# One core, TensorE-bound: the last 64 columns of a weight matrix on both halves of the array, with small loads, stores and the whole order redone

## The chip, the cores and the metric

The kernel runs on one core of one Trainium2 chip. The metric is the device time of the kernel in microseconds (us): a median of several runs. The profiles show one execution each. Engines: PE is TensorE's matmuls, PEld its weight loads, DVE is VectorE, ACT is ScalarE, POOL is GpSimd, SP is SyncE, which here only issues DMAs.

## What is computed

Two branches share a layer norm, and are multiplied and added at the end. S = 2048 rows, D = 640, F = 1728, all in bfloat16.

```python
x  = A_q
xn = layernorm(x)
# A: a 4-tap shift of k, times v, then a long causal convolution along S by FFT
k_shift = sum(k_pad[:, t:t + S, :] * shift_k[:, ks - 1 - t] for t in range(ks))
kv = k_shift * v
y  = irfft(rfft(kv, 2 * S) * rfft(ssm_k, 2 * S))[:S] + kv * ssm_D
s  = xn * y
# B: a feed-forward layer
h  = gelu(xn @ w1 + b1)          # w1: 640 x 1728
g  = silu(h @ w2 + b2)           # w2: 1728 x 640
return x + s * g
```

## The kernel before

Rows of x lie 16 to a partition (partition p holds rows 16p to 16p + 15), which makes 16 groups `n` of 128 rows; four groups make a chunk `c`, so there are four chunks of 512 rows. All row buffers of 640 values are slots of one SBUF tile `mem`; PSUM is one tile `ps` of eight banks.

The order of all work on all engines is one string, `PLAN`. Each word is a step: a name, `/row` for the slot where its result lies, `@bank` for its PSUM bank or banks, and `~a` or `~d` for the engine that evacuates it (ScalarE or VectorE). The steps are recorded in that order, and each engine executes its own instructions in it. The words that matter here:

- Feed-forward, layer 1: `h{c}_{ft}` (`ffn1`, L451) multiplies one tile of 128 columns of w1 (14 tiles, `ft` 0 to 13) with the turned chunk of x, five matmuls of 512 columns that add up over the 640 inputs. In chunk 0 six of the tiles are done in two halves, `ha` and `hb`, of 256 columns. `he` (`ffn1_out`, L456) applies the bias and Gelu into `hT`. F = 1728 is 13 x 128 + 64, so tile 13 holds 64 true columns; the other 64 of its weights are zeros set by `ones_row` (step `mh`).
- Layer 2: `g{c}_{i}` (`ffn2`, L466), 14 matmuls of 320 columns each; i // 2 is the group in the chunk, i % 2 the half of the 640 outputs. The 14th uses 65 rows: 64 of h, and a row of ones against b2, which is row 64 of the last tile of `w2_sb`. Then `ge` (Silu, L471) and `gm` (product with xn, L475).
- Convolution, as a two-stage transform of length 4096 by matmuls: `kf`, `uf` (`mm2`, L197) for the first stage of filter and input, with stores `ks`, `us` to HBM on the POOL queue and loads `fl`, `ml` back on the SP queue; `ff`, `mu` (`mm8`, L207) for the second, `mp` (`product`, L544) the product of the spectra, `mc`, `md` (also L207) back, `ms` a store to HBM, `yl` a load, `y` (`inv2`, L583) the last stage. `mm8` runs one operation as eight matmuls on 32x32 pieces of the array: for each of two halves of the columns, four pieces on one diagonal. The diagonal follows from g: even g use two of the four, odd g the other two.
- Evacuations from PSUM are at L191 (ScalarE) and L192 (VectorE).
- Start: `xl0_0`, `xl0_1` load chunk 0 of x in two halves; `st` (L405, L406) takes the statistics of one group, `sq` and `rc` make the reciprocal root for two groups, `nm` (L421) norms one, `tx` (L426) turns it, `te0_*` evacuates it. `em` (L351) turns the four taps of shift_k, `ee` evacuates them. `wu` and `wv` are matmuls without use that keep TensorE busy.
- k with its shift: `klh` and `kl` load k; row 0 of the three halo slots must be zero, which `k_zero` (steps `kz0` and `kz1`, L280) writes on ScalarE.
- Loads of the feed-forward weights: `wa` (w1 by columns), `wb0` (w2's 13 whole tiles), `wb1` (its last 64 rows, and b2), all on SP.
- End: `yc` (L587) evacuates `y`, `yt` (L592) gates it, `yo` (L598) adds x, and `os` (L603) stores a group, or half of one, on SP.

Of the kernel before, what the change touches and what calls it, by code (L numbers as in the profile page):

```python
# [11 lines left out]
BF16 = mybir.dt.bfloat16  # L12
I32 = mybir.dt.int32
ACT = mybir.ActivationFunctionType
ALU = mybir.AluOpType

P = 128
# [17 lines left out]
ws0/77 st1_1 hb1 h0_13@5 wb1 st1_3 h0_11@2 he0_1 st1_2 xl2/81 h0_10@6 s rs1 kl1 he0_11 h0_12@0 he0_3 he0_2 it0@2  # L35
vl0/85 it1@4 he0_10 hb0 d he0_13 nm1_1 kt1@7 nm1_3 he0_12 kt0@6 nm1_2 em2@5 nm1_0 he0_0 vl1/89 kc1/58~d tt1_0@0
ee2~a ie0/59~d tt1_2@1 tt1_1@7 te1_0/93~d te1_2~a kt8@2 kl2 ss h0_6@5 te1_1~d ie1~d kt2@7 ee3~d kf1_0@0.1 xl3/97
ha4@4 he0_6 kc0/16~d ha5@3 cm0_2/63 hb4 kc2/17~d hb5 cm0_1/101 ke1_0/103~a kf0_0@6.7 h0_8@5 he0_5 cm0_0/105
ke0_0/107~a cm1_0/109 kf2_0@0.1 h0_7@3 he0_8 cm1_1/18 ke2_0/20~a ca0_1 kt9@5 he0_4 kf1_1@6.7 h0_9@0 kc9/22~d ke1_1~a
cm0_3/101 he0_7 kl3 kt3@1 kc8/58~d vl2/65 kt4@4 he0_9 kf2_1@6.7 sm kf0_1@2.3 ke2_1~a ca0_2 g0_0@5 kc3/39~a vl3/0  # L40
cm1_3/4 ke0_1~a ca0_3 kt6@0 ge0_0/0 st2_3 kf3_0@6.7 g0_1@1 st2_1 ke3_0/6~a st2_0 kc4/40~a kt5@5 kt7@2 kc5/17~a
kf3_1@6.7 g0_6@3 st2_2 kc6/16~a ge0_1/1 ca1_1 rs2 ke3_1~a cm1_2/63 kt10@4 ge0_6/2 kf4_1@0.1 kc10/41~a kf4_0@6.7 cv0
g0_3@5 kc7/101~a ks3 nm2_2 nm2_3 ke4_0/18~a nm2_0 ke4_1~a ca1_2 kf5_0@2.3 kf7_0@6.7 kf5_1@0.1 ca1_3 ke7_0/39~a
g0_5@4 cv1 ke5_0/85~a ke5_1~a nm2_1 cm2_1/63 kf7_1@6.7 uf0_0@2.3 gm0_6 g0_4@0 gm0_1 ue0_0/4~a cm2_0/87 ge0_5/2
ke7_1~a cm2_2/6 ge0_3/1 uf1_1@2.3 ks7 ca2_1 uf1_0@6.7 kf6_0@4.5 ks1 cm2_3/101 g0_2@1 ue1_0/63~a ue1_1~a ca2_2
ke6_0/42~a us1 gm0_3 gm0_0 uf2_0@6.7 ge0_4/1 cm3_0/6 ks4 uf0_1@2.3 ge0_2/0 uf3_0@4.5 ks5 ue2_0/39~a ue0_1~d kt14@0
kt15@1 ue3_0/105~a uf3_1@6.7 kc14/17~d kf6_1@2.3 kc15/44~d ue3_1~a kf8_0@4.5 gm0_2 kf8_1@0.1 ke8_0/103~a ke6_1~d
kt11@6 kt12@7 ke8_1~a kc11/110~d kf9_0@4.5 uf2_1@2.3 ca2_3 kc12/16~a kf9_1@0.1 g0_7@6 ke9_0/63~a cv2 ke9_1~a
cm3_1/18 ue2_1~a kf11_0@4.5 ca3_1 ge0_7/0 kf10_1@0.1 kf10_0@2.3 ke11_0/85~a h1_0@7 cm3_3/101 ke10_0/89~a cm3_2/18
ke10_1~a kf11_1@4.5 uf4_0@2.3 he1_0 ke11_1~d h1_1@6 ue4_0/109~d ks11 kf12_0@0.1 uf5_0@4.5 ks0 ca3_2 kt13@2 he1_1  # L50
h1_2@3 us2 ue5_0/45~d ke12_0/18~a ks6 kc13/58~d kf12_1@6.7 ks9 he1_2 kf14_0@4.5 ca3_3 uf4_1@0.1 ks10 ke14_0/22~a
h1_3@2 ke12_1~d us0 ue4_1~a ks2 cv3 uf5_1@4.5 he1_3 it2@3 cm4_1/24 kf13_0@6.7 ue5_1~a kf13_1@0.1 h1_7@2 ke13_0/26~a
cm4_0/28 us5 ke13_1~a us4 cm4_2/30 kf15_0@4.5 uf6_0@6.7 ks13 h1_12@0 cm4_3/32 ue6_0/34~a ks8 ca4_1 ke15_0/36~a us3
it3@1 he1_7 ie2/38~d uf6_1@6.7 ks12 h1_4@4 ue6_1~a ca4_2 ie3~a h1_10@5 ca4_3 he1_4 cv4 uf7_1@2.3 he1_10 uf7_0@6.7
h1_9@1 cm5_1/101 ue7_0/107~a cm5_0/85 ue7_1~a kf15_1@4.5 kf14_1@6.7 cm5_2/87 ke15_1~a h1_5@2 ke14_1~a ca5_1 ks15
h1_8@3 he1_12 ks14 ca5_2 he1_5 us7 uf9_0@4.5 cm5_3/63 he1_8 uf8_0@6.7 us6 h1_11@0 he1_9 ca5_3 ue9_0/4~a h1_6@1 cv5
he1_11 fl0/91 cm6_2/89 fl6/30 h1_13@2 he1_6 fl4/32 gm0_5 fl1/42 ue8_0/109~d uf8_1@4.5 fl3/6 he1_13 uf11_0@0.1 fl2/26
ue8_1~d uf11_1@6.7 fl7/24 ue11_0/65~a tt2_0@3 fl10/44 gm0_4 uf9_1@4.5 ue11_1~a cm6_1/46 uf10_0@0.1 g1_2@2
te2_0/101~a fl12/16 cm6_0/105 ue9_1~a cm7_0/18 fl9/20 ue10_0/87~a ca6_1 ff1@6.7 ff0@4.5 fl8/48 uf10_1@0.1 fe0/36~a
g1_0@3 ca6_2 ge1_2/2 fl5/63 ue10_1~d cm7_1/22 ff12@4.5 ff13@0.1 fe1~a g1_6@2 cm6_3/67 ge1_0/1 ca7_1 fe12/107~a  # L60
fe13~a gm1_0 ca6_3 ff2@6.7 ff3@4.5 ff4@0.1 mk6/95 g1_5@3 cm7_3/93 fe2/34~a fe4/28~a mk0/57 cv6 fe3~a cm7_2/91
fl14/46 uf12_1@6.7 ge1_5/1 mk1/85 uf12_0@0.1 ca7_2 uf13_0@4.5 ue12_0/89~a g1_1@3 gm0_7 fl11/30 ca7_3 ue13_0/50~a
ge1_6/0 cv7 ue12_1~a uf13_1@0.1 st3_2 ff6@4.5 us12 ff7@6.7 g1_3@2 ue13_1~a us11 fe6/22~a st3_0 us8 fe7~a us10 gm1_6
gm1_5 uf14_0@0.1 ge1_3/0 st3_3 uf14_1@4.5 g1_4@6 ue14_0/42~a ue14_1~a gm1_2 st3_1 ge1_1/1 us14 uf15_0@0.1 ge1_4/2
# [24 lines left out]
yl11/30 yl2/32 yl10/18 g3_1@1 yl8/87 ge3_5/1 yl0/89 ge3_2/0 y15@4.5 yl9/91 ge3_1/2 y4@6.7 yc15 gm3_1 y13@0.1 yl7/2
yc4 y14@4.5 yc13 yl5/4 yt4 g3_7@2 yt15 yc14 yo4 yl1/16 ge3_4/2 yt14 yt13 yl6/105 y3@6.7 gm3_2 gm3_4 ge3_7/0 y12@0.1  # L90
# [8 lines left out]
def kernel(  # L99
# [76 lines left out]
    def flat(name, n, o=0):  # L176
        return rows(name, n, o).rearrange("p a b -> p (a b)")
# [490 lines left out]
```

## Time and profile before

| | us |
|---|---|
| median of 3 runs | 202.63 (201.66 to 203.36) |
| the profiled execution | 201.33 |
| its span, first to last instruction | 199.5 |
| granted TensorE clock, mean | 0.994 of full |

| engine | busy us | instructions |
|---|---|---|
| PE | 189.4 (95%) | 2194 |
| DVE | 175.7 (88%) | 304 |
| ACT | 155.1 (78%) | 242 |
| POOL | 39.9 (20%) | 71 |

The profile's page lists busy times, the chain of waits that ended last (followed back from the last instruction), and groups of like instructions with their mean duration and the idle time before them. A line number is that of the kernel; L191, L192, L197 and L207 are helpers that many steps share. Matmuls are pipelined: the mean duration of one (299 ns for 320 columns) is longer than the distance from one start to the next.

### The profile page before, as it was taken

To read this page: it belongs to the slowest core of one execution; us is meant where nothing else is said; L and a number is where in the kernel's file an instruction comes from. 1 tells how busy PE (TensorE), PEld (TensorE's weight loads), DVE (VectorE), ACT (ScalarE), POOL (GpSimd) and SP (SyncE) were. 2 spreads that over 40 slices of the span, in tenths; PEclk is the share of its full clock that TensorE was granted. 3 is DMA by queue.
4 is the path that set the end of the run, shared out by engine and by line. 5 is a ranking of instruction groups with operands and counts; after the bars stand their busy time and mean duration, and the time that the engine had idled before them with its cause. 6 is when DMAs were issued, how large, how long until landed. Compare 5 with 4: busy or idle time off the path is not lost.

```text
span 199.5 us, 5511 instructions
## 1 busy us (share of the span) xinstructions
PE 189.4 (95%) x2194; PEld 114.7 (57%) x2194; DVE 175.7 (88%) x304; ACT 155.1 (78%) x242; POOL 39.9 (20%) x71
## 2 busy tenths in 40 slices
PE   2999999999999999999999999999999999999990
PEld 0685867777766555666743344666654433677760
DVE  7999999999999999999888999888999898009992
ACT  5899999987999998998788778535858767547850
POOL 8402000232308621002620000000062632100000
PEclk9999999999999999999999999999999999999997
DMA  5999999982607979999967999997868492599983
GB/s 209 383 415 334 323 347 405 414 328 75 263 0 276 374 287 320 311 374 324 359 247 225 320 347 375 305 292 292 260 229 306 144 312 89 162 333 402 371 301 137
DMA packets 27120, 57.71 MB, mean 289 GB/s; under 512 B 2966, under 2 KB 16983, under 8 KB 27094
## 3 DMA queue, kind: packets, MB, share of 16 engines
q1 hardware_dynamic: 23072, 41.62, 60.0%
q0 software_dynamic: 3840, 15.73, 21.3%
q8 instruction: 17, 0.28, 0.6%
q14 instruction: 9, 0.07, 0.1%
q10 hardware_dynamic: 182, 0.01, 0.1%
HBM read 33.76 MB, written 18.35 MB: 261 GB/s over the span
## 4 chain that ended last, share of the span: by engine, by line
PE 86%; ACT 3%; issue 3%; DVE 3%; DMA 2%; ACTq 1%; DVEq 0%
PE ps L466 30%; PE ps L451 29%; PE ps L197 9%; PE ps L207 7%; PE ps L583 4%; PE ps L483 3%; ACT mem L191 2%; DMA prm<-in_A_ssm_D_dram 2%; PE ps L432 1%; DVE mem L544 1%; DVE mem L192 1%; PE ps L563 1%; PE ps L351 1%; ACT L471 1%; ACT sl L471 0%
## 5 line engine op out<-in xcount | busy, mean ns | idle before, releaser
L191 ACT CAST mem<-ps 128x640 bf16<-128x640 f32 x101 | 67.0, 699 | 13.8 <-PE ps L207 10.2
L451 PE MATMUL ps<-mem,w_sb 128*128 128x512 bf16 (+1 forms) x310 | 67.8, 359 | 0.4 <-ACT mem L191 0.2
L466 PE MATMUL ps<-w_sb,hT 128*128 128x320 bf16 x448 | 65.8, 299 | 0.2
L466 PEld LDWEIGHTS <-hT 128*128 128x128 bf16 x448 | 42.9, 98 | 18.9 <-issue 1.7
L544 DVE TENSOR_TENSOR mem<-ps,mem 128x1280 bf16<-128x1280 f32 x32 | 46.1, 1486 | 3.6 <-PE ps L207 1.8
L451 PEld LDWEIGHTS <-w_sb 128*128 128x128 bf16 x310 | 28.3, 98 | 27.7 <-issue 4.4
L456 ACT ACTIVATE hT<-ps,b_f 128x512 bf16<-128x512 f32 (+1 forms) x56 | 36.9, 693 | 2.9 <-PE ps L451 2.6
L471 ACT ACTIVATE sl<-ps 128x320 bf16<-128x320 f32 x32 | 13.9, 443 | 16.9 <-PE ps L466 13.6
L502 DVE TENSOR_TENSOR mem<-mem 128x1280 bf16<-128x1280 bf16 x32 | 25.1, 821 | 0.0
L192 DVE CAST mem<-ps 128x640 bf16<-128x640 f32 x27 | 21.7, 821 | 3.0 <-PE ps L207 1.7
L558 POOL DMA_DIRECT2D scrC<-mem x16 | 11.4, 715 | 58.1 <-ACT mem L191 56.5
L207 PE MATMUL ps<-mem,mats 32*32 32x320 bf16 x1024 | 22.6, 300 | 0.4 <-DVE mem L544 0.2
L197 PE MATMUL ps<-mem 128*128 128x320 bf16 x128 | 22.7, 299 | 0.0
L505 DVE TENSOR_TENSOR mem<-mem 128x1280 bf16<-128x1280 bf16 x24 | 19.6, 819 | 0.2
L207 PEld LDWEIGHTS <-mats 32*32 32x32 bf16 x1024 | 9.8, 88 | 15.9 <-issue 13.5
L475 DVE TENSOR_TENSOR mem<-mem,sl 128x320 bf16<-128x320 bf16 x32 | 9.4, 316 | 9.2 <-ACT sl L471 9.0
L197 PEld LDWEIGHTS <-mem 128*128 128x128 bf16 x128 | 12.0, 98 | 5.9
L405 DVE BATCH_NORM_STATS2 stats<-mem 128x6 f32<-128x320 bf16 x32 | 13.6, 468 | 0.0
L518 POOL DMA_DIRECT2D scrU<-mem x16 | 8.7, 545 | 22.3 <-ACT mem L191 21.4
L191 ACT COPY mem<-ps 128x640 bf16<-128x640 bf16 (+2 forms) x16 | 11.4, 746 | 1.7 <-DVE mem L544 0.8
L496 POOL DMA_DIRECT2D scrK<-mem x16 | 8.8, 556 | 19.0 <-ACT mem L191 10.0
L192 DVE COPY mem<-ps 128x640 bf16<-128x640 bf16 (+2 forms) x21 | 11.4, 578 | 0.3 <-PE ps L426 0.3
(75 smaller groups left out, 141.8 us busy)
## 6 DMA issues: line engine op xcount, KB each, us to landing
scrK<-mem POOLq DMA_DIRECT2D x16, 320.0 KB, 3.8
scrU<-mem POOLq DMA_DIRECT2D x16, 320.0 KB, 5.4
mem<-scrK SPq DMA_DIRECT2D x16, 320.0 KB, 6.0
mem<-mem SPq DMA_DIRECT2D x32, 160.0 KB, 5.6
mem<-scrU SPq DMA_DIRECT2D x16, 320.0 KB, 6.8
scrC<-mem POOLq DMA_DIRECT2D x16, 320.0 KB, 4.1
mem<-scrC SPq DMA_DIRECT2D x16, 320.0 KB, 6.5
mem<-in_A_q_dram SPq DMA_DIRECT2D x7, 640.0 KB, 4.6
```

The lines of the kernel that those rows point to most:

```text
L191: return nc.scalar.copy(out=out_ap, in_=in_ap)
L192: return nc.vector.tensor_copy(out=out_ap, in_=in_ap)
L197: nc.tensor.matmul(out=o[:, h, :], lhsT=lhsT, rhs=rhs[:, h * HALF:(h + 1) * HALF], start=start, stop=stop)
L207: nc.tensor.matmul(out=o[j, h, :], lhsT=m[i, i], rhs=rhs[i, h * HALF:(h + 1) * HALF], start=start, stop=stop)
L405: nc.vector.bn_stats(out=stats[:, n, h, :], in_=x_row(n)[:, h * HALF:(h + 1) * HALF])
L451: nc.tensor.matmul(out=bank(hname(c, ft))[:, a:b], lhsT=w1_sb[:, t, ft * P:(ft + 1) * P], rhs=rhs, start=(t == 0), stop=(t == DT - 1))
L456: nc.scalar.activation(out=hT[0:M, ft, :], in_=bank(hname(c, ft))[0:M, :], func=ACT.Gelu_apprx_tanh, bias=b1_f[0:M, ft:ft + 1], scale=1.0)
L466: nc.tensor.matmul(out=bank(f"g{c}_{i}")[:, 0:HALF], lhsT=hT[0:M, ft, q * P:(q + 1) * P], rhs=w2_sb[0:M, ft, hs], start=(ft == 0), stop=(f ...
L471: nc.scalar.activation(out=at["sl", c, i], in_=bank(f"g{c}_{i}")[:, 0:HALF], func=ACT.Silu)
L502: nc.vector.tensor_tensor(out=rows(f"cm{i}_{j}", 2), in0=rows("kz0", 2, 3 + 2 * i - j), in1=taps(j), op=ALU.mult)
L505: nc.vector.tensor_tensor(out=rows(f"cm{i}_0", 2), in0=rows(f"cm{i}_0", 2), in1=rows(f"cm{i}_{j}", 2), op=ALU.add)
L544: nc.vector.tensor_tensor(out=rows(f"mp{g}", 2).rearrange("p k (h c) -> p k h c", h=2), in0=banks(f"mu{g}")[:, None, :, :].to_broadcast([P ...
```

## The change

- Layer 1, tile 13 (`ffn1_last`): the 64 true columns of w1 are loaded twice, into columns 0 to 63 and 64 to 127 of the array. The first copy works on the chunk's first 256 rows of x, the second on the other 256, and the results land in partitions 0 to 63 and 64 to 127 of the bank. `ffn1_out` evacuates that tile by two instructions of 64 x 256.
- Layer 2: for groups 2 and 3 of a chunk the 14th matmul takes all 128 rows: row 0 is ones, rows 1 to 63 zeros (set once by `ones_row`), rows 64 to 127 hold h. `w2_sb` has a 15th tile for it, the last 127 rows of w2 under a row of b2.
- b2 is loaded by two DMAs on POOL's queue (`wb2`); SP's `wb1` loads 64 and 127 rows of w2.
- The halo's zero row is one DMA on SP, from the zero columns of `w1_sb`; the two ScalarE instructions leave.
- Four of the 17 stores of the output (groups 10, 12, 5 and 1) are issued on ScalarE's queue.
- `mm8` takes its pair of diagonals from a table, `SIDE`, that differs from g % 2 for some of the g from 16 on.
- The whole `PLAN` is new: order, slots, banks, and the evacuating engine of some 25 steps. The input loads now begin `xl0_0 xl0_1 xl1 cl0 wa0 cl1`, with `kz0` behind them.

The old and new starts of PLAN, and the core of the rest:

```diff
-io1/0 dm qs xl0_0/8 xl1/12 id pd/16 xl0_1 wa0 wa2 qr cl0/23 cl1 w cl2 io2 wu@0 kz0/39 cl3 st0_0 ws1/58 mh cl4 st0_1
-pt@1 em0@2 wa1 pb sq0 em3@3 kz1 rc0 wv1 nm0_0 nm0_1 tx0@4 st0_2 tx1@5 te0_0/65~a em1@6 klh st0_3 te0_1~a wv1
-ee0/69~a ha2@7 ee1~d ha0@1 sq1 ws2/73 rc1 ha1@0 nm0_2 nm0_3 tx2@2 tx3@6 kl0 te0_2~d ha3@4 te0_3~d st1_0 hb3 wb0 hb2
+io1/0 dm qs xl0_0/8 xl0_1 id pd/12 xl1/34 cl0/38 wa0 qr cl1 w io2 wu@0 st0_0 ws1/19 mh st0_1 pt@1 em0@2 kz0/54 st0_3
+sq0 em1@3 wa2 ee0/73~a cl2 wv3 rc0 st0_2 cl3 cl4 wa1 nm0_0 sq1 ws2/26 rc1 tx0@4 nm0_1 em3@5 nm0_2 tx1@6 te0_0/77~d
+em2@7 nm0_3 tx2@2 te0_1~d tx3@0 pb ha1@4 te0_3~d klh st1_0 ha0@6 ws0/30 ha2@1 kl0 te0_2~d ha3@0 st1_1 hb0 it0@2
...
-g3_6@4 yc6 yo5 os7 yt1 os5 yt6 yo1 yo6 ge3_6/0 os1 os6 gm3_6 yo12_0 yo15_0 os15_0 os12
+gm3_0 os9 y1@6.7 yo13_1 yo12_0 yc6 os14 yt5 g3_6@2 os13 yc1 yt6 yo5 os12~a yt1 os5~a yo6 yo1 ge3_6/0 os6 gm3_6 os1~a
+yo15_0 os15_0
...
+SIDE = "01010101010101011001101000111001"
...
-            turn = 2 * (g % 2) + h
+            turn = 2 * int(SIDE[g]) + h
...
-        nc.gpsimd.memset(hT[FLAST:FLAST + 1, FT - 1, :], 1.0)
+        nc.gpsimd.memset(hT[FLAST:FLAST + 1, FT - 1, 0:2 * P], 1.0)
+        nc.gpsimd.memset(hT[0:FLAST, FT - 1, 2 * P:4 * P], 0.0)
+        nc.gpsimd.memset(hT[0:1, FT - 1, 2 * P:4 * P], 1.0)
...
     def k_zero(i):
-        nc.scalar.activation(out=flat("kz0", 3)[0:1, i * 960:i * 960 + 960], in_=spare[0:1, 0:1].to_broadcast([1, 960]),
-                             func=ACT.Copy, scale=0.0)
+        nc.sync.dma_start(out=flat("kz0", 3)[0:1, :].rearrange("o (a t c) -> o a t c", a=6, t=DT),
+                          in_=w1_sb[0:6, :, F:FT * P])
...
     def load_w2_end():
         nc.sync.dma_start(out=w2_sb[0:FLAST, FT - 1, :], in_=B_w2[(FT - 1) * P:F, :])
-        nc.sync.dma_start(out=w2_sb[FLAST:FLAST + 1, FT - 1, :], in_=B_b2.rearrange("(o d) -> o d", o=1))
+        nc.sync.dma_start(out=w2_sb[1:P, FT, :], in_=B_w2[F - P + 1:F, :])
+
+    def load_b2():
+        for p, ft in ((FLAST, FT - 1), (0, FT)):
+            nc.gpsimd.dma_start(out=w2_sb[p:p + 1, ft, :], in_=B_b2.rearrange("(o d) -> o d", o=1))
...
+    def ffn1_last(c):
+        ft = FT - 1
+        for t in range(DT):
+            for j in range(2):
+                o, s = slice(FLAST * j, FLAST * j + FLAST), slice(2 * P * j, 2 * P * j + 2 * P)
+                nc.tensor.matmul(out=bank(hname(c, ft))[o, s], lhsT=w1_sb[:, t, ft * P:F], rhs=x_turned(c)[:, t, s],
+                                 start=(t == 0), stop=(t == DT - 1))
...
-            M = P if ft < FT - 1 else FLAST + 1
+            up = ft == FT - 1 and q >= 2
+            M = FLAST + 1 if ft == FT - 1 and not up else P
             nc.tensor.matmul(out=bank(f"g{c}_{i}")[:, 0:HALF], lhsT=hT[0:M, ft, q * P:(q + 1) * P],
-                             rhs=w2_sb[0:M, ft, hs], start=(ft == 0), stop=(ft == FT - 1))
+                             rhs=w2_sb[0:M, ft + up, hs], start=(ft == 0), stop=(ft == FT - 1))
...
-    def out_store(n, h=None):
+    def out_store(n, h=None, eng=None):
+        if h == "a":
+            h, eng = None, "a"
         hs = slice(0, D) if h is None else half_of(h)
-        nc.sync.dma_start(out=out_v[:, n, hs], in_=x_row(n)[:, hs])
+        (nc.scalar if eng else nc.sync).dma_start(out=out_v[:, n, hs], in_=x_row(n)[:, hs])
```

More of the change, by code (lines that the diff above doesn't have):

```diff
@@ L36 @@
[L36 to L40, printed above, removed]
@@ new lines @@
+kc2/18~d he0_6 kl1 ie1~d kt1@5 kt5@0 kc1/19~d hb4 kc9/20~d h0_8@1 cm0_0/93 cm1_0/95 kf0_0@6.7 ha5@3 ke0_0/97~a
+cm0_2/99 kf1_0@4.5 hb5 he0_4 kc5/101~d kf2_0@6.7 ke1_0/102~a cm0_1/104 kt7@2 h0_9@0 he0_8 ca0_1 ke2_0/106~a
+kf2_1@4.5 ca0_2 he0_9 kf0_1@6.7 h0_7@1 kl3 cm1_1/108 ke0_1~a he0_5 cm1_3/104 kt10@0 vl2/77 kt4@6 he0_7 kt3@7
+cm1_2/17 g0_0@3 kc7/110~a ca1_1 ke2_1~a kc4/99~a ca1_2 ks2 kc3/100~a kf5_0@4.5 ks0 ca1_3 g0_1@1 ke5_0/56~a st2_3
+ge0_0/0 st2_2 kf1_1@6.7 kf3_0@4.5 g0_6@2 ge0_1/1 st2_0 ke3_0/108~a kc10/17~a vl3/104 st2_1 ke1_1~a kf3_1@4.5
@@ L145 @@
     w1_sb = consts.tile([P, DT, FT * P], BF16, name="w1_sb")
-    w2_sb = consts.tile([P, FT, D], BF16, name="w2_sb")
+    w2_sb = consts.tile([P, FT + 1, D], BF16, name="w2_sb")
     hT = consts.tile([P, FT, CH * P], BF16, name="hT")
@@ L406, in ln_stats, with ln_root @@
         nc.vector.bn_aggr(out=mv[:, n, :], in_=stats[:, n, :, :])
-    def ln_root(c):
-        a, b = c * CH, c * CH + CH
+    def ln_root(a, b):
         nc.gpsimd.tensor_scalar(out=rstd[:, a:b], in0=mv[:, a:b, 1], scalar1=LN_EPS, scalar2=None, op0=ALU.add)
-        nc.gpsimd.tensor_tensor(out=rstd[:, a:b], in0=rstd[:, a:b], in1=mhalf[:], op=ALU.pow)
+        nc.gpsimd.tensor_tensor(out=rstd[:, a:b], in0=rstd[:, a:b], in1=mhalf[:, 0:b - a], op=ALU.pow)
     def ln_sqrt(h):
@@ L452, in ffn1 @@
                              start=(t == 0), stop=(t == DT - 1))
+    def ffn1_last(c):
[5 more added lines that the diff above has]
+                                 start=(t == 0), stop=(t == DT - 1))
     def ffn1_out(c, ft):
-        M = min(P, F - ft * P)
-        nc.scalar.activation(out=hT[0:M, ft, :], in_=bank(hname(c, ft))[0:M, :], func=ACT.Gelu_apprx_tanh,
-                             bias=b1_f[0:M, ft:ft + 1], scale=1.0)
+        for o, s in ([(slice(0, P), slice(0, CH * P))] if ft < FT - 1 else
+                     [(slice(FLAST * j, FLAST * j + FLAST), slice(2 * P * j, 2 * P * j + 2 * P)) for j in range(2)]):
+            nc.scalar.activation(out=hT[o, ft, s], in_=bank(hname(c, ft))[o, s], func=ACT.Gelu_apprx_tanh,
+                                 bias=b1_f[o, ft:ft + 1], scale=1.0)
     def half_of(i):
@@ L626 @@
     }
[L627 removed]
+    G = ("ie0", "ie2") if "ie0/" in PLAN else ("ig0", "ig1")
     with tc.manual_schedule():
```

118 lines of the change are left out of this document (59 added, 59 removed).

## The prediction

> **What bounds the kernel now.** I read the page's busy times first, then the chain of waits in order of time, then the groups with shapes kept apart, and last the timeline of both ends.
>
> ```profile
> span 199.5 us, 5511 instructions
> PE 189.4 (95%) x2194; PEld 114.7 (57%) x2194; DVE 175.7 (88%) x304; ACT 155.1 (78%) x242; POOL 39.9 (20%) x71
> ...
> PE 86%; ACT 3%; issue 3%; DVE 3%; DMA 2%; ACTq 1%; DVEq 0%
> ```
>
> TensorE is busy for 95% of the span and holds 86% of the chain, so I sum its work. The chain gives the price of each kind (start, length, count):
>
> ```profile
> 12.21 0.90 DVE mem L192 x2
> ...
> 23.25 1.08 PE ps L451 x5
> ...
> 32.61 1.90 PE ps L466 x14
> ...
> 110.03 1.19 PE ps L451 x5
> ...
> 143.84 0.90 ACT mem L191 x2
> 144.91 0.73 ACT mem L191
> ...
> 158.13 1.25 DVE mem L544
> ...
> 178.06 2.17 PE ps L583 x16
> ```
>
> 512 columns take 1.08/5 = 0.216 us, 320 columns 1.90/14 = 0.136, so 256 columns 0.109. The same five take 1.19 where work on 32x32 pieces of the array (L207) follows: a change of the array's division costs some 0.10 us. The lines at 144 and 158 show the other thing to see: there the chain leaves TensorE for evacuations and products (L544).
>
> ```profile
> 108.09 0.35 PE L207 MATMUL ps<-mem,mats 32*32 32x320 bf16 x16
> ```
>
> That was the timeline; two groups with shapes apart (name, count, busy us, mean ns):
>
> ```profile
> L207 PEld LDWEIGHTS <-mats 32*32 32x32 bf16 x1024 | 9.8, 88 | 15.9 <-issue 13.5 <-DMA mem<-mem 1.0 <-DMA mem<-scrU 0.4
> L451 PE MATMUL ps<-mem,w_sb 128*128 128x256 bf16 x60 | 7.4, 272 | 0.3 <-ACT mem L191 0.2 <-DVE mem L192 0.2
> ```
>
> Sixteen matmuls of 320 columns end within 0.35 us, where one alone lasts 0.30: pieces in different columns of the array run at once, even on the same rows, and their loads of 88 ns hide.
>
> Before's books: first layer-1 matmul at 10.10, last matmul over at 194.38. In between lie 250 x 0.216 + 60 x 0.109 (layer 1) = 60.5; 448 x 0.136 = 61.0 (layer 2); 192 x 0.136 = 26.1 (L197, L583); 187 transposes of 0.056 to 0.062 = 11.0; 39 runs of 32x32 work, 18.0 by their lengths in the order (0.28 us for two operations of eight matmuls that fill the array together, about 0.13 more for each that meets a busy piece), plus 0.10 each to enter and leave = 4.1. Sum 180.65; the stretch is 184.28, so TensorE waits 3.6 us in all: 0.32 at 12.3 (the chain's line of L192), 1.7 between 139 and 167 by the same counting there, the rest in small pieces. The busy times hide these, since a matmul counts for its full 0.3 us.
>
> ```profile
> 140.00:150.00 10.00, 9.84 (x193) 5.68 (x192) 9.44 (x10) 6.93 (x12) 3.48 (x5) 1.00 0.75 249
> 150.00:160.00 10.00, 9.77 (x169) 4.04 (x168) 9.47 (x8) 7.97 (x13) 4.58 (x8) 1.00 0.64 223
> 160.00:170.00 10.00, 9.95 (x177) 3.81 (x176) 8.96 (x10) 7.00 (x12) 3.00 (x5) 1.00 0.58 202
> ```
>
> (Columns: window, sum, then PE, PEld, DVE, ACT, POOL.) In that stretch VectorE is nearly as full as TensorE: 17 products started 1.40 apart and some 1.9 of other work make 25.7 of 27.2 us.
>
> **The change part by part.**
> *Layer-1's last tile.* Each of four chunks drops 5 x 0.216 = 1.08 and runs 5 pairs of 256 columns, if a pair overlaps, 5 x 0.109 = 0.545. The pairs are a third division of the array. In chunks 0 and 1 full-array work stands on both sides, so two changes (0.10 in, 0.11 out) come new: gain 0.32 each. In chunks 2 and 3 there is 32x32 work on both sides already: gain 0.53 each. Together 1.7. The trace has no 128x64 piece. Bounds: the pair overlaps fully, as L207's pieces do (above); or nothing overlaps and each matmul lasts the 272 ns of its row, 10 x 0.272 = 2.72 a chunk, 8.7 worse in all. I take full overlap, since L207 is the nearest row: same engine, different columns, shared rows.
>
> The Trainium skill ("TensorE: Matmul & The Clock Gate", Part 3, What overlaps and what doesn't) says a weight load overlaps matmuls in flight only when its row group differs, and both halves here use all rows. By its LDWEIGHTS section I estimate 64/1.2 = 53 ns a load, two a pair; that would eat the 1.7 us and 0.4 more. L207's row speaks against it: its loads start while matmuls on the same rows run.
>
> *The new order of 32x32 work* has 40 runs, 18.5 us by the same counting, plus 0.1 for the extra entry: +0.6. The new table SIDE leaves that count as it was within 0.15 (18.4 with the old rule), so I give it nothing; the bound is that 0.15 either way.
>
> *The start.*
>
> ```profile
> 8.08 0.88 DVE L405 BATCH_NORM_STATS2 stats<-mem 128x6 f32<-128x320 bf16 x2
> ...
> 8.76 1.88 ACT L191 COPY mem<-ps 128x640 bf16<-128x640 bf16 x3 [0.75 <-PE ps L426]
> ...
> 10.10 1.80 PE L451 MATMUL ps<-mem,w_sb 128*128 128x256 bf16 x15 [0.17 <-ACT mem L191]
> ```
>
> Before, two rows of x are normed, turned and fed to layer 1 while the other two still wait for their statistics. After, VectorE takes the statistics of rows 3 and 2 first (each 1.04), and itself evacuates the first turned rows. From 6.71, when row 1's statistics are done: 1.0 + 0.17 + 1.04 to 8.9; the second reciprocal after ScalarE's root, 9.47; two norms to 10.25, an evacuation to 10.7, a norm to 11.05, an evacuation to 11.5. Layer 1 starts at 11.52: +1.42. But em2, tx2 and tx3 (0.84) are then already done, and the 0.32 wait at 12.3 goes.
>
> *Zero rows of k by DMA.* Two ScalarE instructions of 0.98 (L280) leave, both from time in which it waited; no gain. Instead SP waits for the memset of w1's zero columns (over at 6.5 in before) with about seven loads issued by 4.0. These hold 2.9 MB, at the 372 GB/s of 10 to 20 us until about 9, so the DMA engines don't run dry and the loads queued behind SP (the rest of w1, filters, k, w2) still go out in time: w1's last columns land at some 11.7 and are used at 15.3, the filters at 15.4 and used at 20.4. Without that cover it is at most 2.5 us.
>
> *b2 on POOL, 127 more rows of w2 on SP.* POOL has only scrK's stores to do after the roots at 18.8, and g0_0, the first user, starts at 33. The extra 160 KB are 0.4 us of DMA time ahead of loads that have 5 us to spare. The two more memsets of hT run on POOL before 8 us, the split Gelu is at most 2 x 0.36 (L471's 0.443 for 320 columns less 64 columns at 1.3 ns, the slope to L456's 694 for 512) for 0.68; ScalarE is 78% busy. Nothing for these; bound +0.2.
>
> *The end.*
>
> ```profile
> 194.41 0.44 ACT L471 ACTIVATE sl<-ps 128x320 bf16<-128x320 f32 x1 [1.11 <-PE ps L466]
> 194.88 0.32 DVE L475 TENSOR_TENSOR mem<-mem,sl 128x320 bf16<-128x320 bf16 x1
> 195.12 0.55 DVE L598 TENSOR_TENSOR mem<-mem 128x320 bf16<-128x320 bf16 x2
> ```
>
> After the last matmul two half-row adds and two stores follow; SP issues the last at 196.09. After the change row 12's add comes earlier and its store goes out on ScalarE's queue: one add, one store, issued at about 195.47. Gain 0.62. Four stores now stand in ScalarE's order; one (row 5) waits for VectorE just ahead of the last Silu. By before's times that add is done at 193.7 and the issue by 194.2, before the Silu is due; if it is late, the gain is gone.
>
> **The sum.** First layer-1 matmul +1.42; TensorE's work after it: -4.32 (20 matmuls of 512 columns) + 2.60 (pairs with their drain) + 0.6 - 0.84 = -1.96; wait at 12.3 -0.32; end -0.62; the other 3.3 us of waits unchanged. Total -1.48: span 198.05, profiled time 201.33 to 199.85. Over the median 202.63, which stands 1.3 above the profiled run, that is 201.1, 0.7% less.
>
> **The rivals.**
> *Waits shrink too.* VectorE's listed work falls by 1.9 us (evacuations moved to ScalarE), and the 3.3 us of waits are evacuations and products. For it: DVE 9.4 of 10 where they lie. Against: 25.7 of 27.2 us there must be done anyway, and those 17 products stay, so no more than 1.5 goes: 201.1 - 1.5 = 199.6.
> *New waits.* Every evacuation has a new place; a product that comes one place late costs 1.40. If waits double, 201.1 + 3.3 = 204.4. Against: that order keeps the ratio of the engines in each stage.
> *The halves don't overlap* (slower). One after the other, 2 x 0.109 a pair: 2.2 lost, 203.3. With bare loads too, 10 x (0.109 + 0.098) = 2.07 a chunk for 0.545: 6.1 lost, 207.2, slower than before. From 0.18 us a pair on it is no gain, from 0.28 more than 1% slower. For it: no such piece in the trace; against: L207. The skill's rule above is the middle case, loads bare and halves overlapping, 201.1 + 2.1 = 203.2.
>
> **How the numbers follow.** Forecast 0.45, with a range of its own of 200.0 to 202.3 (start 0.3, end 0.6, half of the chunk savings lost where VectorE binds); waits shrink 0.24; new waits 0.16; no overlap 0.15, half of it as bare loads. A measurement of this kernel tells about 1% from none. Under 200.6 lie the shrinking waits and 0.18 of the forecast: faster 0.42. Over 204.7: half of the new waits, the bare loads and some of the rest of no overlap, 0.20. Within 1%: 0.38. Range 198.9 to 204.7: the shrinking waits with 0.7 for the spread of runs, up to the doubled waits; bare loads stay out.
>
> **What would show it.** Right: L462's layer 1 starts near 11.5; five pairs of 64 columns take near 0.55 us, the two halves starting within 10 ns; last matmul near 193.5; the last store issued 1.1 us after it. Wrong: pairs 0.2 us or more apart, a chain with more VectorE or DMA in it between 139 and 167, ScalarE's last Silu held by a store, or SP's wait showing as late filters at 20 us.

## The result, and the profile after

The change made the kernel slower. Median 204.42 us (202.98 to 206.58, 20 runs) against 201.68 us (201.12 to 203.36, 20 runs) for the kernel before; ratio 1.0116, 95% interval 1.0089 to 1.0143. The forecast was 0.7% less. Ratios leave out slow executions (more than 1.5% above the fastest of their kernel, most of them at a lower clock), so a ratio need not equal that of two medians; the run with 128 rows alone (below) keeps five of its ten, and its profile is of one left out.

The page of the changed kernel (its profiled execution took 205.35 us, clock 0.999):

```profile
span 203.6 us, 5562 instructions
PE 189.9 (93%) x2215; PEld 114.8 (56%) x2215; DVE 174.5 (86%) x303; ACT 155.5 (76%) x245; POOL 41.6 (20%) x75
...
PE 56%; DMA 23%; DVE 5%; SPq 5%; POOL 3%; ACT 3%; issue 2%; POOLq 0%; DVEq 0%; ACTq 0%
```

TensorE held 86% of the chain that ended last, DMA 2%; now it is 56% and 23%. A share of the chain is not time lost, but it says where to look: transfers have come onto the path. The chain in order of time (start, length, what) says which:

```profile
15.73 7.64 SPq L390
23.90 16.28 DMA mem<-in_A_q_dram
...
112.22 6.50 DMA mem<-scrU
...
178.74 6.80 DMA mem<-scrC
185.60 7.21 DMA mem<-scrC
```

The issue at L390 (w2's last rows) is nothing new: in the kernel before it was held 8.21 us from 14.73 on. But x's third chunk (`xl2`) takes 16.28 us from issue to landing, and further on a `ml` load and two `yl` loads stand in the chain. The forecast's own books, redone for both profiles (first layer-1 matmul, TensorE's work after it, its waits, and what follows the last matmul; "mended" is the kernel with four loads mended and `pt` moved, the fastest of the experiments):

| us | before | forecast | after | mended |
|---|---|---|---|---|
| first layer-1 matmul | 10.10 | 11.52 | 12.89 | 11.38 |
| work after it | 180.64 | 178.68 | 178.68 | 178.68 |
| waits | 3.63 | 3.31 | 7.99 | 4.44 |
| after the last matmul | 5.15 | 4.53 | 4.01 | 3.94 |
| span | 199.5 | 198.05 | 203.6 | 198.4 |

The miss is 1.4 us of start and 4.7 us of waits, less 0.5 us at the end. The work is counted by the forecast's price list, and the waits are what is left of the stretch, so the agreement of the work is not evidence by itself. One comparison needs no list: from layer 1 on, the changed and the mended kernel run the same matmuls in the same order, and the distances from each start to the next differ by 3.55 us in all, of which 2.4 lie between 45 and 60 us, 0.7 near 118 and 0.45 near 192.

**The start.** Timelines of ScalarE and TensorE (start, length, engine, line; in brackets the idle time before and its releaser):

```profile
1.86 0.70 ACTq L259 DMA_DIRECT2D prm<-in_B_b_dram  x1
...
8.14 0.17 PE L366 MATMUL ps<-ident,prm 19*128 19x19 bf16 x1 [2.11 <-DMA prm<-in_A_ssm_D_dram]
```

In the kernel before:

```profile
6.42 0.17 PE L359 MATMUL ps<-ident,prm 19*128 19x19 bf16 x1 [0.39 <-DMA prm<-in_A_ssm_D_dram]
```

L366 (L359 before) is `pt`, the transpose of the parameters. It stands ahead of every tap and row in TensorE's order, and waited 2.11 us for the last parameter load, 0.39 before. The load of b1's last 64 values, now doubled by a repeating source, took 0.70 us to issue (0.23 before).

**The middle.** SP's timeline, in the changed kernel and then in the kernel before, and one window (busy time by engine, granted clock, DMA share, GB/s):

```profile
23.41 0.44 SPq L391 DMA_DIRECT2D w_sb<-in_B_w_dram  x1
23.90 7.01 SPq L377 DMA_DIRECT2D mem<-in_A_q_dram  x1
```

```profile
23.46 0.34 SPq L370 DMA_DIRECT2D mem<-in_A_q_dram  x1
```

```profile
30.00:32.00 2.00, 2.00 (x18) 1.38 (x16) 1.97 (x4) 2.00 (x4) 0.00 (x0) 1.00 0.44 81
```

L391 is the load of 127 rows, L377 (L370 before) is `xl2`, held 7.01 us at issue behind it, where the kernel before needed 0.34. The DMA engines move 81 GB/s between 30 and 32 us and 249 on average from 30 to 37; in the kernel before that average was 406. In the trace's packets the 127 rows go out from 31 to 38 us at 14 to 21 a microsecond of 55 to 76 ns each: their times add up to 1.04 to 1.16 us in each microsecond, so one engine's worth: the load went out as if on one of the 16 engines. The Trainium skill ("DMA: Bandwidth & Descriptors", section on why a DMA increments its semaphore by 16) states the rule: a DMA is spread over the largest number up to 16 that divides the slowest dimension of both its sides, and it names 127 partitions as an example that gets one engine. The packets agree.

What waits for it, as groups with shapes apart (name, count, busy, mean | idle before, releaser), in 40 to 60 us and in 105 to 125 us:

```profile
L417 DVE BATCH_NORM_STATS2 stats<-mem 128x6 f32<-128x320 bf16 x8 | 3.4, 465 | 2.6 <-DMA mem<-in_A_q_dram 2.6
```

```profile
L210 PE MATMUL ps<-mem,mats 32*32 32x320 bf16 x280 | 6.2, 301 | 0.9 <-DMA mem<-scrU 0.8
```

VectorE's statistics of the third chunk wait 2.6 us, and what stands behind them in VectorE's order makes TensorE wait 2.7 us between 44 and 58. The second line is `mu2`, waiting for `ml1`.

**The stretch that I feared** is nearly as it was; 2.2 us of waits between 140 and 170 by the same counting, against 1.8 before:

```profile
140.00:150.00 10.00, 9.47 (x214) 5.75 (x212) 8.86 (x10) 6.63 (x11) 0.74 (x1) 1.00 0.73 235
150.00:160.00 10.00, 9.80 (x169) 4.80 (x164) 9.92 (x9) 7.27 (x12) 3.62 (x5) 1.00 0.89 296
160.00:170.00 10.00, 9.75 (x195) 3.82 (x193) 9.52 (x8) 7.41 (x13) 4.34 (x6) 1.00 0.58 199
```

**The end.** One of ScalarE's stores, the last Silu behind it, and the last add:

```profile
198.86 0.34 ACTq L627 DMA_DIRECT2D out_dram<-mem  x1
...
199.60 0.44 ACT L493 ACTIVATE sl<-ps 128x320 bf16<-128x320 f32 x1 [1.10 <-PE ps L488]
...
200.43 0.32 DVE L620 TENSOR_TENSOR mem<-mem 128x320 bf16<-128x320 bf16 x1
```

One add follows the last product (two before), the Silu is not held by a store, and the last store is issued at 200.78, 1.22 us after the last matmul (1.71 before).

### The profile page after: what moved, and what is told of

Its sections match the earlier page's. It is cut to its first block, busy times and chain, and to the rows that moved or that the text cites. A ratio compares the mean times of both kernels' runs of the same rounds, so it can differ in the third digit from the quotient of the medians.

```text
span 203.6 us, 5562 instructions
## 1 busy us (share of the span) xinstructions
PE 189.9 (93%) x2215; PEld 114.8 (56%) x2215; DVE 174.5 (86%) x303; ACT 155.5 (76%) x245; POOL 41.6 (20%) x75
## 4 chain that ended last, share of the span: by engine, by line
PE 56%; DMA 23%; DVE 5%; SPq 5%; POOL 3%; ACT 3%; issue 2%; POOLq 0%; DVEq 0%; ACTq 0%
PE ps L488 20%; PE ps L462 17%; DMA mem<-in_A_q_dram 8%; PE ps L210 8%; DMA mem<-scrC 7%; PE ps L200 7%; DMA mem<-in_A_ssm_k_dram 4%; SPq L390 4%; DMA mem<-scrU 3%; ACT mem L194 2%; DVE stats L417 2%; DMA scrC<-mem 1%; PE ps L605 1%; POOL ident masks.py:199 1%; SPq L598 1%
## 5 line engine op out<-in xcount | busy, mean ns | idle before, releaser
L194 ACT CAST mem<-ps 128x640 bf16<-128x640 f32 x103 | 68.2, 701 | 14.1 <-PE ps L210 8.1
L462 PE MATMUL ps<-mem,w_sb 128*128 128x512 bf16 (+1 forms) x290 | 63.1, 358 | 0.3
L477 ACT ACTIVATE hT<-ps,b_f 128x512 bf16<-128x512 f32 (+1 forms) x60 | 38.1, 664 | 5.3 <-PE ps L462 4.9
L462 PEld LDWEIGHTS <-w_sb 128*128 128x128 bf16 x290 | 26.5, 98 | 25.1 <-issue 3.4
L200 PE MATMUL ps<-mem 128*128 128x320 bf16 x128 | 23.4, 299 | 1.7 <-DVE mem L530 0.9
L210 PE MATMUL ps<-mem,mats 32*32 32x320 bf16 x1024 | 23.2, 301 | 1.7 <-DMA mem<-scrU 0.8
L195 DVE CAST mem<-ps 128x640 bf16<-128x640 f32 x25 | 20.2, 821 | 3.1 <-PE ps L210 2.8
L497 DVE TENSOR_TENSOR mem<-mem,sl 128x320 bf16<-128x320 bf16 x32 | 10.0, 319 | 10.9 <-ACT sl L493 10.7
L609 ACT CAST mem<-ps 128x640 bf16<-128x640 f32 x16 | 10.4, 706 | 3.2 <-PE ps L605 3.0
```

The lines of the kernel that those rows point to most:

```text
L194: return nc.scalar.copy(out=out_ap, in_=in_ap)
L195: return nc.vector.tensor_copy(out=out_ap, in_=in_ap)
L200: nc.tensor.matmul(out=o[:, h, :], lhsT=lhsT, rhs=rhs[:, h * HALF:(h + 1) * HALF], start=start, stop=stop)
L210: nc.tensor.matmul(out=o[j, h, :], lhsT=m[i, i], rhs=rhs[i, h * HALF:(h + 1) * HALF], start=start, stop=stop)
L462: nc.tensor.matmul(out=bank(hname(c, ft))[:, a:b], lhsT=w1_sb[:, t, ft * P:(ft + 1) * P], rhs=rhs, start=(t == 0), stop=(t == DT - 1))
L477: nc.scalar.activation(out=hT[o, ft, s], in_=bank(hname(c, ft))[o, s], func=ACT.Gelu_apprx_tanh, bias=b1_f[o, ft:ft + 1], scale=1.0)
```

## The experiments

**Does the load of 127 rows cost the middle?** The changed kernel with that load in 128 rows; b2's row is written over row 0 afterwards.

```diff
-        nc.sync.dma_start(out=w2_sb[1:P, FT, :], in_=B_w2[F - P + 1:F, :])
+        nc.sync.dma_start(out=w2_sb[0:P, FT, :], in_=B_w2[F - P:F, :])
```

> The changed kernel with one difference: the 15th tile of w2 is loaded by 128 rows instead of 127 (row 0 is overwritten with b2 afterwards). Theory A (127 rows go to one DMA engine: in the changed kernel's trace 14 to 20 packets of 1280 bytes per us trickle from 29 to 38 us, SP's next issue, x's third chunk, takes 7.0 us, and that chunk lands at 40.2): with 128 rows that issue takes under 1 us, the chunk lands before 36, VectorE's 2.6 us wait for it and TensorE's 2.9 us of waits between 44 and 58 go, and the span falls from 203.6 to about 200.7. Rival B (it is the 160 KB more in the line, or SP's earlier waits): same volume, so the issue still takes about 7 us and the span stays within 0.7 of 203.6.

Median 204.14 (201.61 to 209.81), ratio 0.9987 (0.9948 to 1.0025). SP's timeline and the window:

```profile
22.58 0.58 SPq L391 DMA_DIRECT2D w_sb<-in_B_w_dram  x1
23.21 0.92 SPq L377 DMA_DIRECT2D mem<-in_A_q_dram  x2
```

```profile
30.00:32.00 2.00, 2.00 (x16) 1.30 (x15) 1.93 (x3) 2.00 (x4) 0.50 (x1) 1.00 1.05 399
```

`xl2` and `xl3` are now issued in 0.92 us together, the DMA engines move 399 GB/s, `xl2` lands at 32.6 instead of 40.2, and TensorE's waits between 44 and 58 fall from 2.7 to 0.3. The changed kernel's loss is gone, but no more than that. In this profile the waits at 110 to 120 rose to 4.2, since `ml1` landed at 117.8, against 118.73 in the changed kernel, while TensorE had come there 2.8 us earlier (issue, time to landing):

```profile
109.61 8.17 DMA mem<-scrU
```

That wait is 2.7 us here and 1.0 in the profile with two loads mended (below), so its size in this profile is not typical.

**The reverse: that load alone in the kernel before**, where nothing reads what it brings.

```diff
+        nc.sync.dma_start(out=w2_sb[1:P, FT, :], in_=B_w2[F - P + 1:F, :])
```

> The kernel before with one load more on SP, between b2 and x's third chunk: 127 rows of w2 into a tile that nothing reads (the change's load alone). If the 127 rows run on one DMA engine, as the changed kernel's trace has it, x's third chunk is issued some 6 us long and lands near 40 instead of 34, TensorE waits 2 to 3 us between 44 and 58, and the time is 1.5 to 2.8 us more: ratio 1.007 to 1.014. Rival (only together with the change's order, which uses that chunk earlier, is it late): ratio within 0.997 to 1.004.

Median 205.42 (204.60 to 205.62, 4 runs), ratio 1.0155 (1.0118 to 1.0192), so 3.1 us, more than was expected. `xl2` was held 5.16 us at issue and landed at 38.3; VectorE waited for it more than in the changed kernel, and TensorE's waits between 40 and 60 went from 0.15 to 4.05. In the window 36 to 60:

```profile
L406 DVE BATCH_NORM_STATS2 stats<-mem 128x6 f32<-128x320 bf16 x8 | 3.4, 465 | 4.0 <-DMA mem<-in_A_q_dram 4.0
```

This load alone costs as much as the whole change (1.0116), or more; the intervals overlap.

**The doubled load of b1, alone in the kernel before.**

```diff
-nc.scalar.dma_start(out=prm[FT - 1:FT, 0:FLAST], in_=B_b1[(FT - 1) * P:F].rearrange("(o p) -> o p", o=1))
+nc.scalar.dma_start(out=prm[FT - 1:FT, :].rearrange("o (a p) -> o a p", a=2),
+    in_=B_b1[(FT - 1) * P:F].rearrange("(o a p) -> o a p", o=1, a=1).to_broadcast([1, 2, FLAST]))
```

> The kernel before with b1's last 64 values loaded twice by one load that repeats its source, as the change does (the second copy is read by nobody). If that load makes the parameters late: issue 0.70 instead of 0.23 us, pt near 7.2 instead of 6.4 to 6.8, layer 1 some 0.5 later, ratio 1.001 to 1.004. Rival (the bytes issued ahead of them decide): pt at 6.4 to 6.8, ratio 0.998 to 1.001.

Median 203.31, ratio 1.0041 (1.0012 to 1.0070), 0.8 us. Issue took 0.70 us and `pt` started at 7.77, layer 1 at 11.45 instead of 10.10. The profiles of all runs with the same loads up to there scatter, though: `pt` started at 6.42, 6.58 and 6.79 with one plain load, at 7.16 and 7.77 with the doubled one, and from 6.83 to 8.64 in the new order with the doubled one (seven profiles). With plain loads in the new order (below) it was 6.62, 6.83 and 7.53, so there the effect of the doubled load does not stand out of the scatter.

**Do bytes ahead of the parameters make them late?** 128 rows, and `wa0` issued ahead of `xl1` and `cl0`.

```diff
-pd/12 xl1/34 cl0/38 wa0 qr cl1
+pd/12 wa0 xl1/34 cl0/38 qr cl1
```

> The changed kernel with tile 15 of w2 in 128 rows, and with the first part of w1 (wa0) issued on SP ahead of xl1 and cl0, so that the bytes issued before the parameter loads of ScalarE's queue are those of the kernel before. Theory A (the parameters are late since their small packets run behind xl1 and cl0): pt starts near 6.8 instead of 7.5 to 8.1, layer 1 at 11.5 to 11.8 instead of 12.3 to 12.9. Rival B (the doubled load of b1, issued in 0.70 instead of 0.23 us, makes them late by itself): pt stays at 7.4 or later. Either way most of the gain would be lost again at ml1, which is left in its late place: time 203 to 204.5, ratio 1.003 to 1.012.

`pt` stayed at 7.49, layer 1 at 12.72; median 204.05, ratio 1.0046 (1.0004 to 1.0089). Theory A failed: with the old bytes ahead of them the parameters did not land earlier (7.45 in the next run but one, which has the same move). This profile shows the `yl` loads instead, 2.1 us of waits between 180 and 190.

**The place of `ml1`.** 128 rows, `ml1` right behind `ml0`.

```diff
-ml0/6 fe9~d fe5~a ml8/106 ... ff24@6.7 ml1/32 ff22@0.1
+ml0/6 ml1/32 fe9~d fe5~a ml8/106 ... ff24@6.7 ff22@0.1
```

> The changed kernel with tile 15 of w2 loaded in 128 rows, and with the load ml1 moved from eighth to second among the loads on SP that follow ml0. In the run with 128 rows alone, ml1 was issued at 110.1, landed at 118.7, the same moment as in the changed kernel (118.73), and TensorE waited 2.7 us there before h2_13 and mu2 (0.9 in the changed kernel): what the 128 rows saved at 44 to 58 us was mostly given back behind ml1. Theory A (ml1's place in SP's order ends that stretch): ml1 lands near 110.5, the waits at 110 to 120 fall from 4.2 to under 1.5, the time is 1.5 to 3 us less than with 128 rows alone (204.1), so 201 to 202.5, ratio to the kernel before 0.992 to 1.002. Rival B (the next load in the queue, ml8 or a swapped copy mk0, is as late and takes ml1's place): waits there stay over 3 us, ratio 1.005 to 1.012.

Median 202.76, ratio 0.9987 (0.9944 to 1.0030), the ratio of the 128 rows alone: no gain in time that can be told. (The landing at 118.7 that the text above gives for the run with 128 rows is that of the load behind `ml1`; `ml1` itself landed at 117.8 there, as its chain shows.) `ml1` now landed at 107.05, and the waits at 110 to 120 are 1.0 us. They did not go: the block of `mu4` began at 113.64, just as `ml2` had landed (113.60), which now stood behind `ml1`. The profile puts the 0.49 us of idle time before that block down to ScalarE, so `ml2` as its cause is an inference.

**All three.**

> All three repairs: tile 15 of w2 in 128 rows, ml1 second behind ml0, wa0 ahead of xl1 and cl0. If the theory is right that these three loads are what the prediction missed, the pairs, the earlier row 12 and the repaired loads together give: first layer-1 matmul 11.6, work after it 178.7, waits near 4.5, tail 4.0, so a span near 198.8 and a time of 199.5 to 201.5, ratio 0.985 to 0.997: faster than the kernel before. Rival (the order's waits move on to the products between 140 and 170 whenever something ahead of them gets earlier): waits of 6 us or more, ratio 0.998 to 1.006.

Median 203.06, ratio 1.0027 (0.9988 to 1.0065): a miss. Waits of 6.2 us, of which 1.25 at 110 to 120 and 0.7 at 180 to 190. The rival had that number, but not the place: between 140 and 170 the waits are no longer than in the other profiles of this order. They are at loads again.

**Four loads mended in the order of use.** 128 rows; b1's 64 values by two plain loads; the first ten loads behind `scrU`, and the last seven behind `scrC`, in the order in which TensorE needs them (the changed order had `yl0` behind `yl1` and `yl9`, though `y0` comes first).

```diff
-ml0 ml8 mk2 mk0 ml15 ml2 ml12 ml1 ml4 mk1
+ml0 ml2 mk2 mk0 ml1 ml8 mk1 ml15 ml12 ml4
-yl8 yl1 yl9 yl0 yl7 yl6 yl5
+yl8 yl0 yl7 yl9 yl5 yl6 yl1
```

> The changed kernel with four things about its loads mended: tile 15 of w2 in 128 rows; the first ten loads behind scrU's stores in the order in which TensorE uses them (ml0, ml2, mk2, mk0, ml1, ml8, mk1, ml15, ml12, ml4); the last seven yl loads likewise (yl8, yl0, yl7, yl9, yl5, yl6, yl1, where yl0 stood behind yl1 and yl9); b1's last 64 values by two plain loads instead of one that repeats its source. Theory A (what the prediction missed is loads in the wrong place of a queue): the waits at 103 to 122 us fall from 1.4 to under 0.8, those at 175 to 193 from 0.7 to under 0.3, pt starts near 6.8, layer 1 near 11.5; span 198 to 199, time 199.5 to 201, ratio to the kernel before 0.985 to 0.995. Rival B (the DMA engines are full between 103 and 131 and between 174 and 188, so another load is late when one is helped): waits in these two stretches as in the run with three repairs, 2 us together, ratio 0.998 to 1.005.

Median 201.09 (200.13 to 202.91), ratio 0.9948 (0.9914 to 0.9983): 0.5% less than the kernel before. Waits 4.7 us, 0.4 at 110 to 120, none at 180 to 190, as theory A had it. But layer 1 began at 13.15 in this profile (11.5 expected), `pt` at 7.53.

**Are the two odd loads all?** The changed kernel with the 128 rows and the two plain loads only.

> The changed kernel with its two suspect loads alone mended: tile 15 of w2 in 128 rows, b1's last 64 values by two plain loads. Alone in the kernel before these two loads cost 1.55% (127 rows) and 0.41% (the doubled b1), 1.96% together; the whole change costs 1.16%. Theory A (they are all that the prediction missed): the rest of the change is worth 0.8%, ratio 0.990 to 0.995, the forecast's 0.993. Rival B (in the new order other loads, ml1 and the last yl loads, are late as well and take a part back): ratio 0.997 to 1.004, as the runs with 128 rows and the doubled b1 had it (0.999 to 1.005).

Median 202.68, ratio 1.0004 (0.9978 to 1.0029): rival B. The `ml` load is late by itself; in 105 to 125:

```profile
L210 PE MATMUL ps<-mem,mats 32*32 32x320 bf16 x268 | 5.9, 302 | 1.1 <-DMA mem<-scrU 1.0
```

So mending the two odd loads takes 1.1% of time out of the changed kernel, and the order of the loads another 0.6% (0.9948 against 1.0004; the two intervals just overlap). The 128 rows alone had come to 0.9987, so in this order the plain loads of b1 add nothing that can be told. Layer 1 began at 12.12 here although `pt` was at 6.83: the chain has `wa0` landing at 12.08. It was issued at 4.51, behind an earlier load, and at 2.10 in the kernel before.

**`pt` behind the rows.** The four mended loads, and `pt` moved behind `tx3`, where its result is first needed.

```diff
-st0_1 pt@1 em0@2 ... tx2@2 te0_1~d tx3@0 pb
+st0_1 em0@2 ... tx2@2 te0_1~d tx3@0 pt@1 pb
```

> The kernel with the four mended loads, and the transpose of the parameters (pt) moved on TensorE from ahead of em0 to behind tx3, just before layer 1, where its result is first needed. If late parameters set the start of layer 1 only since pt stands first in TensorE's order, the start no longer depends on when they land: em0 begins near 6, layer 1 at 11.0 to 11.6 (before the move 13.15 with pt at 7.53), and the time falls by 0.5 to 1.5 us under the 201.1 of the four loads: ratio to the kernel before 0.987 to 0.992. Rival (the first rows of x, their statistics on VectorE and their norms set it anyway): layer 1 at 12 or later, ratio 0.993 to 0.997.

Median 200.65 (200.19 to 201.82), ratio 0.9930 (0.9902 to 0.9958), the lowest of all. The time fell by 0.4 us, less than the 0.5 to 1.5 that was expected, and the interval overlaps that of the four loads, so the gain of this move in time is not shown; its effect on the start is. The shares of its page's chain, and the chain up to layer 1:

```profile
PE 88%; DVE 6%; ACT 2%; issue 1%; POOL 0%; DVEq 0%; POOLq 0%
```

```profile
7.82 0.80 DVE stats L417 x2
...
9.21 0.17 DVE rstd L428
9.38 0.70 DVE mem L432 x2
10.08 0.40 DVE mem L195
10.47 0.37 DVE mem L432
```

DMA is out of the chain's shares, and the start is now the chain of VectorE that the forecast wrote down: reciprocal over at 9.38 (forecast 9.47), two norms at 10.08 (10.25), an evacuation at 10.47 (10.7), a norm at 10.84 (11.05), layer 1 at 11.38 (11.52). The one other profile with this move (the last one of the next part) has layer 1 at 11.45.

**What the pairs are worth.** In four kernels layer 1's last tile was put back to five matmuls of 512 columns a chunk, its Gelu in one piece:

```diff
-"h": lambda c, ft: ffn1(c, ft) if ft < FT - 1 else ffn1_last(c)
+"h": ffn1
```

The changed kernel:

> The changed kernel with layer 1's last tile as before, five matmuls of 512 columns, one Gelu of 64 rows; loads, order and all else stay. If the pairs are worth what their records show (0.67 us to the next matmul against 1.08 to 1.18), this is slower than the changed kernel by up to 1.7 us: span 203.6 to 205.3. Rival (savings fall into TensorE's waits for loads and products): chunk 0's and 2's and 3's tiles stand ahead of waits, so only part appears, 0.3 to 0.9: span 203.9 to 204.5.

The one with three repairs:

> The kernel with the three repaired loads, with layer 1's last tile again as five matmuls of 512 columns in each chunk (its Gelu in one piece). TensorE's work is 1.7 us more. If nothing else is late, pairs are worth those 1.7 us here: time 1.2 to 2 us above the run with pairs, ratio between the two about 0.992. Rival: in the changed kernel the same edit moved the time by nothing that could be told, as TensorE then waited less; if that comes from the products that set the pace between 140 and 170, it holds here too and the two are within 0.5 us.

The one with four mended loads:

> The kernel with the four mended loads, with layer 1's last tile as five matmuls of 512 columns a chunk. Theory A: with loads in the order of use the pairs' 1.7 us reach the end, time 1 to 2 us above the run with pairs. Rival B: the two within 0.5 us, with TensorE's waits about 1.7 us smaller than in the run with pairs, as it was with three repairs (3.8 against 6.3).

That one with `pt` moved:

> The kernel with the four mended loads and pt behind tx3, with layer 1's last tile as five matmuls of 512 columns a chunk. If the pairs' 1.7 us reach the end now that the start is 11.4 and the waits 4.4: ratio 0.999 to 1.003 (0.993 with the pairs), waits near 4.4 again. If TensorE's waits behind the products and loads take them up, as in the changed kernel and with three repairs: waits near 3, ratio 0.993 to 0.997.

| | with pairs | without | work | waits with, without |
|---|---|---|---|---|
| changed | 1.0116 | 1.0093 (1.0060 to 1.0125) | +1.7 | 8.0, 3.5 |
| three repairs | 1.0027 | 1.0004 (0.9964 to 1.0045) | +1.7 | 6.2, 3.8 |
| four mended | 0.9948 | 0.9968 (0.9932 to 1.0003) | +1.7 | 4.7, 3.5 |
| and `pt` | 0.9930 | 0.9953 (0.9928 to 0.9977) | +1.7 | 4.4, 3.6 |

(Ratios to the kernel before.) Without the pairs TensorE's work is 1.7 us more in each, by the count. In the first two rows the time does not rise with it; with the loads mended it rises by 0.2%, about 0.5 us, which no single interval tells from nothing. Where the rest goes is shown only in part, since each entry of the last column is one profile. In the last two, 0.8 of the 1.7 us is waits that the kernel without pairs does not have. In the first row most of the difference is not the pairs' doing: with the same load of 127 rows ahead of it, `xl2` was held 5.54 us instead of 7.01 and landed at 38.4 instead of 40.2, layer 1 began 0.7 us later, and TensorE's waits between 40 and 60 were 0.3 us instead of 2.7. What that load costs the changed kernel thus differs from one execution to another.

**The pairs alone in the kernel before** (w2's 15th tile here by 64 rows and a memset, b2 by POOL, the doubled b1 with them):

> The kernel before with the pairs alone: its own order, k's zeros on ScalarE, all stores on SP; the 15th tile of w2 gets 64 rows on SP, zeros by a memset and b2 on POOL's queue. Theory (the pairs are a gain, the new order's loads the loss): span falls by 0.32 in chunks 0 and 1 and up to 0.53 in 2 and 3, to 197.8 if all appears, 198.9 if the two in the stretch where VectorE binds do not. Rival (pairs cost as much as they save, by drains and two Gelus): 199.5, within 0.5.

Median 202.74, ratio 1.0035 (1.0011 to 1.0059). Work fell by 1.72; `pt` at 7.16 and layer 1 0.75 later, and waits rose from 3.6 to 6.2: the span of 201.1 missed theory and rival. The doubled b1 alone comes to 1.0041, so the pairs themselves are worth nothing that can be told here.

**The end alone in the kernel before** (row 12's add earlier, three stores on ScalarE's queue):

> The kernel before with only its end changed: row 12's add ahead of the last layer-2 tile, stores of rows 12, 5 and 1 on ScalarE's queue. Prediction's step: the last store is issued 0.6 us earlier and the span is 0.6 shorter, 198.9. Rival (the changed kernel's end is 4.0 us after the last matmul against 5.1 for other reasons; the landing of the stores ends the span whatever queue issued them): 199.5 within 0.2.

What follows the last matmul fell from 5.15 to 4.54, by 0.61 (forecast 0.62). Only 0.43 of that is the earlier issue of the last store, 1.28 us after the last matmul instead of 1.71. Median 202.11, ratio 0.9975 (0.9945 to 1.0005): in the time the gain is not told from none.

## Why the prediction was wrong, step by step

**The pairs: right in work, too large in time.** The five pairs started 106 to 130 ns apart with 3 to 4 ns between the halves, and tile 13 took 0.67 us with its drain (forecast 0.545 and 0.11). The rule of the Trainium skill ("TensorE: Matmul & The Clock Gate", Part 3, on what overlaps), by which a weight load overlaps matmuls in flight only when its row group differs, does not hold for these halves: both use all rows, yet the second pair's loads begin 27 to 30 ns after the first pair's matmuls, which last 277. The loads lasted 106 to 111 ns each, twice the estimate of 53, and hid. L207 was the right row to go by. But the sum booked the 1.7 us as time, and the runs with mended loads show some 0.5.

**The new order of 32x32 work and SIDE: not tested apart.** The 178.68 us of work are the forecast's count of the same steps, and no run changes SIDE alone. What they are worth stays open.

**The start: the chain right, waits for loads missing.** The sum followed x through VectorE and took it that the parameters land as before. It named `pt` nowhere, though `pt` leads TensorE's order and had 4.17 us of a DMA before it in the old chain. The doubled load costs 0.41% by itself in the kernel before. The start's miss of 1.4 us lies within the scatter of that landing (`pt` from 6.83 to 8.64 with the same loads), and with `pt` moved layer 1 began at 11.38 and 11.45. The sum had no term for `wa0` either, which set the start at 12.12 in one profile.

**"127 more rows of w2 on SP ... 160 KB are 0.4 us of DMA time": the step that failed.** It priced bytes at the rate of 16 engines. The load went out at the rate of one, its last packets some 14 us behind its issue; it held SP's next issue 7 us and let `xl2` land 7.6 us later than the load in 128 rows did. Put alone into the kernel before it costs 3.1 us, and mended together with the doubled load it takes 1.1% out of the changed kernel. The prediction's bound for this and three other small terms together was 0.2 us, and its cover of "5 us to spare" was not measured against a load that blocks its queue. The signs of being wrong that it listed look at the stretch from 139 to 167, the end and the filters; none looks at the loads between 23 and 60 us.

**k's zero row and b2: right.** SP's wait for the memset put `wa2` 3.2 us back (7.56 for 4.34), yet between the start of layer 1 and 40 us TensorE waited 0.3 us at most in any profile of the new order. b2's rows landed at 25.3 and 25.7 without a wait shown for them.

**"The other 3.3 us of waits unchanged": failed, for another reason than the rivals had.** The rival of doubled waits gave 204.4, and 204.42 was measured, but its mechanism was evacuations and products in a new place. Those 30 us wait as they did (2.2 against 1.8). What came late were loads: `xl2`, as told above; `ml1`, which moved from third to eighth among the loads from `ml0` on and landed 12.5 us after `ml0`'s issue instead of 5.8; `yl0` and `yl7`, behind loads used after them. The text treated SP's queue at the start only and never compared its order at 105 and 175 us with TensorE's. With all these mended, waits are 4.4 to 4.7.

**The end: right, a little small.** 0.5 us is the shorter work ahead of the last store (forecast 0.62); from the last store's issue to the end of the span it also took 0.65 less, which no step of the prediction explains. The four stores on ScalarE's queue did not hold the last Silu.

With the four loads mended and `pt` moved the ratio is 0.9930, the forecast's own 0.7%. That agreement is partly luck: the start and the end came out a little better than the sum, the waits 1.1 us worse.

## What to carry to other kernels

Price a DMA by how many engines its shape can use before pricing its bytes: 127 rows can turn 160 KB into a blocked queue, where 128 rows, of which one is overwritten, did not. When an order is made anew, put the order of the loads in each queue beside the order in which the consumers use them, in every stage; here a load that slipped a few places behind others cost TensorE up to 1.0 us at one place. And do not book work that leaves the busiest engine as time: of 1.7 us no more than some 0.5 appeared here, and only once the loads were mended.

## What the runs showed that was not expected

- A load of 127 rows of 1280 bytes: one engine's worth of packet time for over 7 us, and the next load on that queue held 7.01 us at issue (5.54 in another execution with the same loads, 5.16 with this load added to the kernel before); behind 128 rows, 0.43.
- A load of 128 bytes repeated twice by its source took 0.70 us to issue; two plain loads took 0.23 and 0.27.
- Two 64-column halves of the array that share all rows start 3 to 4 ns apart, and pairs follow each other in 106 ns for 256 columns (130 from the first to the second).
- TensorE's first use of the same small parameter loads comes up to 1.8 us apart from one profile to another (6.83 to 8.64). Whether that makes most of the scatter of the kernel's time is not shown.
